# An attention and two-MLP kernel: w3 turned by VectorE and by its store instead of by TensorE, and other sharing of banks and slots in the last stage

## The chip, the cores and the metric

The kernel runs on one NeuronCore of one Trainium2 chip. A core has TensorE (PE, matrix products), VectorE (DVE), ScalarE (ACT), GpSimd (POOL) and SyncE (SP, which here only issues DMAs) and PSUM of eight banks that PE writes and DVE and ACT read. Sixteen DMA engines move data between HBM and SBUF. The metric is device time of one execution in microseconds (us).

## The reference

```python
# q, k, v: 4 x 8 heads x 576 x 64; a causal window of 64 keys
x = softmax(q k^T / 8, windowed) v        # -> 2304 tokens x 512
g = x @ w_gate; v = x @ w_val             # 512 x 1536 each
x = (silu(g) * v) @ w_out                 # 1536 x 512 -> 2304 x 512
a = x @ w1; b = x @ w2                    # 512 x 1024 each
out = ((a * b) @ w3) @ w_out2             # 1024 x 1024, then 1024 x 512
```

The weights come as 64-bit floats and are made 32-bit ones on the chip. The product of the last line is computed as (a * b) @ (w3 @ w_out2), so that w3 meets the 2304 tokens in no product: w34 = w3 @ w_out2 is 1024 x 512.

## The kernel before

**Number format.** Every operand of a matmul is two words, a rounded one (hi, cast on ACT, L197) and the remainder (lo, a subtraction on DVE, L201), and every product takes three passes: hi x hi, hi x lo, lo x hi (`PASSES`).

**Stages in order of time** (the profile's clock): attention (to about 120 us); the first gated MLP; `project`, the product with w_out, in three groups of 768 tokens (PE from 385 to 535 us, three groups of equal work; groups change at 435 and 485 us); the second gated stage (a and b); and `final` from 711 us, the only stage whose code changes, though its weight w3 is prepared earlier.

**How w3 is prepared.** `Plain` (L1012 on) loads 128 rows of w3 in 64-bit form (`st_w`, 1 MB), four instructions for each half narrow it (DVE L185, DVE L187, ACT L189, DVE L191), an ACT copy (L1030) takes the result into a tile `by_w` of 128x512, and a DMA (L1049) stores it to a scratch in HBM, `w3d`. There are eight such row blocks, each in two halves. Four blocks are prepared in `project` (stores at 435, 457, 462 and 468 to 470 us), four in the second gated stage (582 to 648 us). All DMAs are issued by SP, in one queue, in program order; each waits for the one eight before it.

**The first half of `final`: w34.** For each of eight row blocks i (order 0, 4, 1, 5, ...) `transposes(n)` loads the block from `w3d` (L758, two DMAs of 256 KB), turns it on PE against the identity (L771, eight 128x128 pieces into three banks `w3p`), casts it from PSUM on ACT (L773) and takes the remainder on DVE (L774). `row(n)` then runs 24 matmuls of 128x512 (L883, `acc`) of the turned block against the tiles z0h to z7l (w_out2 in two words, sixteen loads of 256 KB, L750). Block n + 1 is turned before row n, so two blocks are turned ahead of the first row. `Right` makes operands of the result: sums and words of the pieces of w34, for seven products.

**The second half of `final`: the output.** For each of three groups of 768 tokens (`Group`), seven products in the order 1, 2, 5, 6, 7, 4, 3 (`PRODUCTS`, a Strassen-Winograd scheme) of 36 matmuls of 128x256 (L948) each, 12 for each of three 128-token tiles t. Products 1, 6, 7 and 4 go into the banks `al` (one for each t), product 2 into `ga` and products 5 and 3 into `be`. After product 1 each `al` is copied to SBUF by ACT (L918); after product 2 each `ga` is added by DVE (L922, 128x256); after 6, 7 and 4 ACT copies `al` again, and after 7 and 3 DVE adds `be`. `ga` has three results in two banks: t = 0 and 1 share one bank, t = 2 has the other. The left operands `hf` of product p and piece m are made by `Left` from the loaded h tiles: for products 5, 6, 7 and 4 first a DVE subtraction in place (L205), then cast (L197) and remainder (L201). `Left` of the next group is queued at product 5.

**What sets the order.** A planner (`Plan`) writes each engine's instructions in a fixed order while the kernel is built. It keeps its own clock with costs such as `dve(n) = 0.16 + 0.00104 n` us, and emits a queued job on an engine when its inputs are due by that clock. `plan.slots` counts free SBUF slots; a job that needs one waits in the queue until `slots` exceed `plan.keep`. On the chip each engine runs its instructions in the written order and waits by semaphores: an instruction that is late holds up everything written behind it on its engine.

Of the kernel before, what the change touches and what calls it, by code (L numbers as in the profile page):

```python
# [16 lines left out]
P = 128  # L17
# [15 lines left out]
def window_attention_moe_kernel(ctx: ExitStack, tc: tile.TileContext, q, k, v, w_gate, w_val, w_out, w1, w2, w3, w_out2, out):  # L33
# [702 lines left out]
    def final(rows, ident):  # L736
# [4 lines left out]
        zt, w3t, w3T = {}, {}, {}  # L741
# [11 lines left out]
        def queue_w3(n):  # L753
            i = ROWS[n]
            for x in range(2):
                def load(eng, x=x):
                    w3t[i, x] = slot([P, 512], F32, f"w3_{i}_{x}")
                    eng.dma_start(out=w3t[i, x], in_=w3d[i][:, 512 * x:512 * x + 512])  # L758
                jobs["w3", i, x] = loading(load, [done[n - 3]] if n > 2 else (), 1)

        def transposes(n):
            i = ROWS[n]
            w3T[i] = []
            for x in range(2):
                plan.need(jobs["w3", i, x])
            for g in range(0, NI, 3):
                n_ = min(3, NI - g)
                pt = bank(f"w3p{i}_{g}")[:, :n_ * P]
                for c in range(n_):
                    at = divmod((g + c) * P, 512)  # L770
                    nc.tensor.transpose(pt[:, c * P:c * P + P], w3t[i, at[0]][:, at[1]:at[1] + P], ident)  # L771
                t = slot([P, 2, T], F32R, f"w3T{i}_{g}")
                nc.scalar.copy(out=t[:, 0, :n_ * P], in_=pt)  # L773
                nc.vector.tensor_tensor(out=t[:, 1, :n_ * P], in0=pt, in1=t[:, 0, :n_ * P].bitcast(F32), op=ALU.subtract)  # L774
                plan.charge("ACT", act(n_ * P))
                plan.charge("DVE", dve(n_ * P))
                w3T[i].append(t)
            plan.slots += 2
            reach(done[n])
# [52 lines left out]
        class Left:  # L832


            def __init__(self, tp):
# [35 lines left out]
                def gone(eng):  # L871
                    plan.slots += NI
                plan.job(gone, [j for x in last.values() for j in x], SP=0.0)
# [3 lines left out]
        def row(n):  # L877
            i = ROWS[n]
            acc = bank(f"acc{i}")
            for c in range(NI):  # L880
                for k, (x, y) in enumerate(PASSES):
                    plan.need(jobs["z", c, y])
                    nc.tensor.matmul(acc, lhsT=w3T[i][c // 3][:, x, (c % 3) * P:(c % 3) * P + P], rhs=zt[c, y],  # L883
                                     start=c == k == 0, stop=c == NI - 1 and k == 2)
                plan.advance(0.68)
            right.put(i, acc)
# [15 lines left out]
        class Group:  # L902
# [28 lines left out]
            def product(self, p):  # L931
# [3 lines left out]
                if p == 1:  # L935
                    self.al = [bank(f"al{self.tp}_{t}")[:, :N2] for t in range(3)]
                elif p == 2:
                    two, one = bank(f"ga{self.tp}_0"), bank(f"ga{self.tp}_1")
                    self.ga = [two[:, :N2], two[:, N2:], one[:, :N2]]
                elif p == 5:  # L940
                    self.be = [bank(f"be{self.tp}_{t}")[:, :N2] for t in range(3)]
# [30 lines left out]
        def run():  # L972
            transposes(0)
            for n in range(NI):
                if n + 1 < NI:
                    transposes(n + 1)
                if n == 3:
                    left[0] = Left(0)
                row(n)
            plan.slots += 2 * NI  # L980
            plan.keep = 6
            for tp in range(NTP):
                group = Group(tp)
                for p in PRODUCTS:
                    if p == 5 and tp + 1 < NTP:
                        left[tp + 1] = Left(tp + 1)
                    group.product(p)
# [29 lines left out]
    class Plain(Doubles):  # L1017
# [6 lines left out]
        def make(self):  # L1024
            for j, ready in enumerate(self.narrowed()):
                t = []

                def copy(eng, j=j, t=t):
                    t.append(large([P, 512], F32, f"by_{self.name}_{j}"))
                    eng.copy(out=t[0], in_=halves(self.st[:, 512 * j:512 * j + 512])[1].bitcast(F32))  # L1030
                a = plan.job(copy, [ready] + by[-2:-1], ACT=act(512))
                self.last.append(a)
                by.append(plan.job(lambda eng, j=j, t=t: self.put(eng, self.n, j, t[0]), [a], lag=5.0, SP=0.5))
# [6 lines left out]
    w3d = [dram.tile([P, DF2], F32, name=f"w3d_{i}") for i in range(DF2 // P)]  # L1040
# [7 lines left out]
    def put_w3(eng, i, j, t):  # L1048
        eng.dma_start(out=w3d[i][:, 512 * j:512 * j + 512], in_=t)  # L1049
# [125 lines left out]
    with tc.manual_schedule():  # L1175
        attention(during_attention)
        ident2 = own.tile([P, P], F32, name="ident2")
        nc.gpsimd.memset(ident2, 1.0)
        nc.gpsimd.affine_select(out=ident2, in_=ident2, pattern=[[-1, P]], compare_op=ALU.is_equal, fill=0.0,
                                base=0, channel_multiplier=1)  # L1180
# [8 lines left out]
        begin_e, run_e = final(rows2, ident2)  # L1189
# [39 lines left out]
```

## Time and profile before

| | |
|---|---|
| median of 3 runs | 864.48 us (863.35 to 864.81) |
| the profiled execution | 863.41 us, of which the span from the first to the last instruction is 861.7 us |
| granted TensorE clock, mean over the span | 0.998 of full speed |
| PE busy | 831.9 us, 97% of the span |
| DVE, ACT, POOL busy | 636.9 us (74%), 458.2 us (53%), 86.0 us (10%) |
| DMA queue | 135.29 MB, 47.7% of 16 engines over the span |

An engine's busy time is the union of its instructions; matmuls are pipelined, so one matmul is in flight longer (334 ns for one of 128x384) than the time between two (about 172 ns). "Idle before, releaser" says which instruction ended a wait. The chain of waits follows the run back from its last instruction; where a stage's chain holds only PE, that stage takes as long as its matmuls.

### The profile page before, as it was taken

Reading aid. Unit: us, or ns where it says so; the run is one execution under the profiler, and the core shown is the slowest. Engines: PE = TensorE matmul, PEld = TensorE weight load, DVE = VectorE, ACT = ScalarE, POOL = GpSimd, SP = SyncE. Lnnn points to the kernel's source line nnn. Section 1 sums busy time; section 2 is a strip of 40 time slices with the busy share of each in tenths; the row PEclk is TensorE's granted clock in tenths of the full one; section 3 lists DMA queues with packets and bytes.
Section 4 is the critical chain, followed back from the end, with each engine's and each line's share of the span. In section 5 each row is a group of like instructions: output and inputs, shape, how many; then the busy total and the mean of one; then the engine's idle time right before and its main releaser. Section 6 shows DMA issues by size and latency. Waiting matters only on the chain.

```text
span 861.7 us, 15759 instructions
## 1 busy us (share of the span) xinstructions
PE 831.9 (97%) x5934; PEld 798.3 (93%) x5934; DVE 636.9 (74%) x1332; ACT 458.2 (53%) x1192; POOL 86.0 (10%) x119
## 2 busy tenths in 40 slices
PE   7899888899999999999999999999999999999998
PEld 6777677899999999999999999999999998899998
DVE  4899968878688767875797683877788645688683
ACT  6888855564646464643565543445454424556362
POOL 3688930000000000000000000000000000000000
PEclk9999999999999999999999999999999999999999
DMA  9979200135255324599997341023545179042422
GB/s 201 221 164 198 80 1 38 41 123 185 108 194 209 143 79 178 184 349 391 384 329 233 135 125 46 37 86 111 196 159 195 50 251 383 1 147 75 147 75 74
DMA packets 109756, 136.30 MB, mean 158 GB/s; under 512 B 61424, under 2 KB 72432, under 8 KB 108656
## 3 DMA queue, kind: packets, MB, share of 16 engines
q1 hardware_dynamic: 109680, 135.29, 47.7%
q8 instruction: 47, 0.77, 0.4%
q14 instruction: 29, 0.24, 0.1%
HBM read 92.27 MB, written 42.99 MB: 157 GB/s over the span
## 4 chain that ended last, share of the span: by engine, by line
PE 80%; DVE 8%; DMA 4%; ACT 2%; SPq 2%; issue 2%; POOL 2%; POOLq 0%; ACTq 0%; DVEq 0%
PE ala L578 14%; PE alb L578 14%; PE o L718 14%; PE beb L578 7%; PE bea L578 7%; PE al L948 6%; PE acc L883 5%; PE gab L578 4%; PE gaa L578 3%; PE be L948 3%; DMA zd<-by_z 2%; PE ga L948 1%; DVE ptt L449 1%; SPq L347 1%; DMA st_z<-in_moe_w_out_dram 1%
## 5 line engine op out<-in xcount | busy, mean ns | idle before, releaser
L718 PE MATMUL o<-ph,wo 128*128 128x384 f32 x576 | 146.5, 334 | 0.2 <-DVE X L705 0.2
L718 PEld LDWEIGHTS o<-ph,wo 128*128 128x128 f32 x576 | 104.1, 188 | 0.5 <-ACT by_w L1030 0.5
L718 PE MATMUL o<-pl,wo 128*128 128x384 f32 x288 | 96.2, 334 | 0.0
L585 ACT COPY ha<-ala 128x384 f32<-128x384 f32 x90 | 42.8, 478 | 54.8 <-PE ala L578 53.3
L589 DVE TENSOR_TENSOR ha<-ha,bea 128x384 f32<-128x384 f32 x60 | 33.2, 554 | 46.4 <-PE bea L578 27.1
L718 PEld LDWEIGHTS o<-pl,wo 128*128 128x128 f32 x288 | 54.1, 188 | 0.0
L424 ACT ACTIVATE pexp<-S,stat 128x128 f32<-128x128 f32 x144 | 51.8, 397 | 0.0
L197 ACT CAST hf<-h 128x384 fp32r<-128x384 f32 x84 | 39.0, 518 | 19.0 <-DVE h L205 18.9
L599 ACT ACTIVATE ha<-ha 128x384 f32<-128x384 f32 x54 | 28.3, 526 | 38.4 <-DVE ha L589 38.4
L201 DVE TENSOR_TENSOR pl<-pl,ph 128x768 fp32r<-128x768 f32 x36 | 33.8, 956 | 19.1 <-ACT ph L197 18.8
L434 POOL TENSOR_TENSOR pexp<-pexp,stat 128x384 f32<-128x384 f32 x48 | 44.4, 944 | 26.7 <-DVE stat L431 21.7
L201 DVE TENSOR_TENSOR hf<-h,hf 128x384 fp32r<-128x384 f32 x84 | 43.2, 554 | 3.4 <-ACT hf L197 3.3
L197 ACT CAST ph<-pl 128x768 fp32r<-128x768 f32 x36 | 29.2, 838 | 27.8 <-DMA pl<-h 20.8
L585 ACT COPY c12b<-alb 128x384 f32<-128x384 f32 x30 | 14.4, 481 | 49.4 <-PE alb L578 49.2
L589 DVE TENSOR_TENSOR c22b<-c22b,beb 128x384 f32<-128x384 f32 x30 | 16.6, 555 | 26.4 <-ACT c22b L585 26.2
L424 ACT ACTIVATION_READ_ACCUMULATOR pexp<-S,stat 128x1 f32 x144 | 33.9, 236 | 0.0
L417 DVE TENSOR_REDUCE stat<-S 128x3 f32<-128x384 f32 x48 | 24.3, 546 | 6.2 <-PE S L410 6.1
L578 PE MATMUL ala<-xo,w_g_1h 128*128 128x384 f32 x120 | 27.0, 337 | 1.7 <-ACT w_g_1h L197 1.7
L463 PEld LDWEIGHTS PV<-ptt,v 128*64 128x64 f32 x576 | 19.5, 137 | 9.2 <-DVE ptt L449 4.5
L463 PE MATMUL PV<-ptt,v 128*64 128x64 f32 x576 | 22.9, 228 | 5.1 <-DVE ptt L449 4.0
L918 ACT COPY o<-al 128x256 f32<-128x256 f32 x36 | 13.4, 373 | 26.3 <-PE al L948 24.9
L201 DVE TENSOR_TENSOR xo<-X,xo 128x384 fp32r<-128x384 f32 x37 | 22.6, 641 | 5.6 <-ACT xo L197 5.6
(546 smaller groups left out, 2524.4 us busy)
## 6 DMA issues: line engine op xcount, KB each, us to landing
h<-ha SPq DMA_DIRECT2D x60, 384.0 KB, 3.2
pl<-h SPq DMA_DIRECT2D x36, 384.0 KB, 6.4
h<-h SPq DMA_DIRECT2D x24, 384.0 KB, 4.8
st_w<-in_moe_w_dram SPq DMA_DIRECT2D x8, 1024.0 KB, 6.8
st_g<-in_moe_w_gate_dram SPq DMA_DIRECT2D x6, 1024.0 KB, 5.6
st_v<-in_moe_w_val_dram SPq DMA_DIRECT2D x6, 1024.0 KB, 5.4
st_wo<-in_moe_w_out_dram SPq DMA_DIRECT2D x6, 1024.0 KB, 5.3
wo<-by_wo SPq DMA_DIRECT2D x12, 512.0 KB, 3.7
```

The source lines that it names most:

```text
L197: (eng.copy if eng is nc.scalar else eng.tensor_copy)(out=hi(), in_=src())
L201: return plan.job(lambda eng: eng.tensor_tensor(out=lo(), in0=src(), in1=hi().bitcast(F32), op=ALU.subtract), after, slots=slots, DVE=dve( ...
L424: nc.scalar.activation(out=pe[:, jj, :], in_=so[:, jj, :], func=AF.Exp, bias=st[:, 0, x, jj:jj + 1], accum_out=st[:, 1, x, jj:jj + 1])
L434: nc.gpsimd.tensor_tensor(out=pe, in0=pe, in1=st[:, 3, x, :].unsqueeze(2).to_broadcast([P, SUB, P]), op=ALU.mult)
L463: nc.tensor.matmul(pp[64 * h:64 * h + 64, 64 * (SUB * x + jj):64 * (SUB * x + jj) + 64], lhsT=vt[u][e][:, at, h, :], rhs=t[:, x, jj, c:c + ...
L578: nc.tensor.matmul(acc, lhsT=self.wt.ops[p, x][:, m, :], rhs=self.xs.ops[p, m][:, y, :], start=start and n == 0, stop=n == 5, skip_group_c ...
L585: nc.scalar.copy(out=out, in_=src)
L589: nc.vector.tensor_tensor(out=out, in0=x, in1=y, op=ALU.add)
L599: nc.scalar.activation(out=h, in_=src, func=func)
L718: nc.tensor.matmul(acc[m, x], lhsT=wos.tiles[i // 6][:, i % 6, :], rhs=rows[2 * tp + x].words(f, b), start=f == n == 0, stop=f == NF - 1 a ...
L883: nc.tensor.matmul(acc, lhsT=w3T[i][c // 3][:, x, (c % 3) * P:(c % 3) * P + P], rhs=zt[c, y], start=c == k == 0, stop=c == NI - 1 and k == 2)
L948: nc.tensor.matmul(acc, lhsT=self.xs.ops[p, m][:, x, t * P:t * P + P], rhs=right.ops[p, m, y], start=start and n == 0, stop=n == 3 * R - 1 ...
```

## The change

1. w3 is turned as it is prepared: the ACT copy into `by_w` becomes a DVE transpose of 128x512 that turns each 32x32 square in itself (L1022 of the new kernel), and the store (L1042) puts the squares in their turned places: four DMAs for each half, each of 64 KB in 512 runs of 128 bytes (one run is one row of a square), into rows of 4096 bytes of one 1024x1024 scratch. Before it was one DMA of 256 KB for each half, in runs of 2048 bytes.
2. In `final` the loads (L762) bring the turned block straight into the operand's slot, three DMAs of 192, 192 and 128 KB for each row block in runs of 512 bytes; the cast and the remainder are now queued jobs (L197, L201) that read SBUF. The 64 transposes on PE, their banks, and the identity that POOL made for them are gone.
3. `ga`: t = 0 and t = 2 share one bank, t = 1 has the other.
4. `Left` gives its slots back in two halves and not all at once, the next group's `Left` is queued at product 6 and not 5, and `plan.keep` is 3 and not 6 in the products.
5. The planner counts 2.0 us of SP and 6.0 us of landing for a store of w3, before 0.5 and 5.0.

```diff
-    def final(rows, ident):
+    def final(rows):
...
         def queue_w3(n):
+
             i = ROWS[n]
-            for x in range(2):
-                def load(eng, x=x):
-                    w3t[i, x] = slot([P, 512], F32, f"w3_{i}_{x}")
-                    eng.dma_start(out=w3t[i, x], in_=w3d[i][:, 512 * x:512 * x + 512])
-                jobs["w3", i, x] = loading(load, [done[n - 3]] if n > 2 else (), 1)
-
-        def transposes(n):
-            i = ROWS[n]
-            w3T[i] = []
-            for x in range(2):
-                plan.need(jobs["w3", i, x])
+            w3T[i] = [None] * -(-NI // 3)
             for g in range(0, NI, 3):
-                n_ = min(3, NI - g)
-                pt = bank(f"w3p{i}_{g}")[:, :n_ * P]
-                for c in range(n_):
-                    at = divmod((g + c) * P, 512)
-                    nc.tensor.transpose(pt[:, c * P:c * P + P], w3t[i, at[0]][:, at[1]:at[1] + P], ident)
-                t = slot([P, 2, T], F32R, f"w3T{i}_{g}")
-                nc.scalar.copy(out=t[:, 0, :n_ * P], in_=pt)
-                nc.vector.tensor_tensor(out=t[:, 1, :n_ * P], in0=pt, in1=t[:, 0, :n_ * P].bitcast(F32), op=ALU.subtract)
-                plan.charge("ACT", act(n_ * P))
-                plan.charge("DVE", dve(n_ * P))
-                w3T[i].append(t)
-            plan.slots += 2
-            reach(done[n])
+                k = min(3, NI - g)
+
+                def load(eng, g=g, k=k):
+                    t = w3T[i][g // 3] = slot([P, 2, T], F32R, f"w3T{i}_{g}")
+                    eng.dma_start(out=t[:, 1, :k * P].bitcast(F32).rearrange("p (c f) -> p c f", c=k),
+                                  in_=w3d[P * g:P * (g + k), P * i:P * i + P].rearrange("(c p) f -> p c f", p=P))
...
+                a = loading(load, [done[n - 3]] if n > 2 else (), 1)
+                b = cast(lambda word=word: word(0), lambda word=word: word(1).bitcast(F32), [a], k * P, 0)
+                jobs["w3", i, g // 3] = rest(lambda word=word: word(1), lambda word=word: word(1).bitcast(F32),
+                                             lambda word=word: word(0), [b], k * P)
...
                 def gone(eng):
-                    plan.slots += NI
-                plan.job(gone, [j for x in last.values() for j in x], SP=0.0)
+                    plan.slots += R
+                for p in (4, 3):
+                    plan.job(gone, [j for (q, m), x in last.items() if q in (7, p) for j in x], SP=0.0)
...
                     two, one = bank(f"ga{self.tp}_0"), bank(f"ga{self.tp}_1")
-                    self.ga = [two[:, :N2], two[:, N2:], one[:, :N2]]
+                    self.ga = [two[:, :N2], one[:, :N2], two[:, N2:]]
...
-            plan.keep = 6
+            plan.keep = 3
             for tp in range(NTP):
                 group = Group(tp)
                 for p in PRODUCTS:
-                    if p == 5 and tp + 1 < NTP:
+                    if p == 6 and tp + 1 < NTP:
                         left[tp + 1] = Left(tp + 1)
...
-                    eng.copy(out=t[0], in_=halves(self.st[:, 512 * j:512 * j + 512])[1].bitcast(F32))
-                a = plan.job(copy, [ready] + by[-2:-1], ACT=act(512))
+
+                    eng.transpose(out=t[0], in_=halves(self.st[:, 512 * j:512 * j + 512])[1].bitcast(F32))
+                a = plan.job(copy, [ready] + by[-2:-1], DVE=dve(512))
...
 def put_w3(eng, i, j, t):
-        eng.dma_start(out=w3d[i][:, 512 * j:512 * j + 512], in_=t)
+        for a in range(P // 32):
+            eng.dma_start(out=w3d[512 * j:512 * j + 512, P * i + 32 * a:P * i + 32 * a + 32].rearrange("(b p) f -> p b f", p=32),
+                          in_=t[32 * a:32 * a + 32].rearrange("p (b f) -> p b f", f=32))
```

The written order moves with it, at three places that matter below. The first is DVE in `project`, where the first group of tokens ends (435 us in the profile of before): `st_w` is the block of w3 being narrowed, `pl` and `ph` are left operands of `project`, and the four L705 copies empty banks `o` that PE needs for the next group. Before, and then now:

```order
L201 TENSOR_TENSOR pl_1_0_5210<-pl_1_0_5210,ph_1_0_5290 128x768
L185 TENSOR_SCALAR st_w_5217<-st_w_5217 128x512 x2
L187 SCALAR_TENSOR_TENSOR st_w_5217<-st_w_5217 128x512 x2
L191 SCALAR_TENSOR_TENSOR st_w_5217<-st_w_5217 128x512 x2
L705 COPY X_0_0_4921<-o_0_0_4925 128x384
L705 COPY X_0_1_4922<-o_1_0_4927 128x384
L705 COPY X_0_2_4923<-o_2_0_4929 128x384
```

```order
L201 TENSOR_TENSOR pl_1_0_5200<-pl_1_0_5200,ph_1_0_5280 128x768
L185 TENSOR_SCALAR st_w_5207<-st_w_5207 128x512 x2
L187 SCALAR_TENSOR_TENSOR st_w_5207<-st_w_5207 128x512 x2
L191 SCALAR_TENSOR_TENSOR st_w_5207<-st_w_5207 128x512 x2
L1022 STREAM_TRANSPOSE by_w_0_5318<-st_w_5207 128x512
L1022 STREAM_TRANSPOSE by_w_1_5320<-st_w_5207 128x512
L705 COPY X_0_0_4911<-o_0_0_4915 128x384
L705 COPY X_0_1_4912<-o_1_0_4917 128x384
```

Two transposes now stand between the narrowing and the copies that empty the banks.

The second is DVE in the products of the first group of `final`, from product 7 to product 4: `hf_4m` are the operands of product 4, `o_1t` the additions of `be` after product 7. Before, and then now:

```order
L201 TENSOR_TENSOR hf_40_8795<-h_0_4_8254,hf_40_8795 128x384
L205 TENSOR_TENSOR h_0_7_8284<-h_0_7_8284,h_0_3_8279 128x384
L922 TENSOR_TENSOR o_10_8756<-o_10_8756,be_0_8675 128x256
L201 TENSOR_TENSOR hf_33_8640<-h_0_7_8284,hf_33_8640 128x384
L922 TENSOR_TENSOR o_11_8774<-o_11_8774,be_1_8676 128x256
L922 TENSOR_TENSOR o_12_8791<-o_12_8791,be_2_8677 128x256
L201 TENSOR_TENSOR hf_41_8843<-h_0_5_8264,hf_41_8843 128x384
L201 TENSOR_TENSOR hf_42_8845<-h_0_6_8274,hf_42_8845 128x384
L201 TENSOR_TENSOR hf_43_8848<-h_0_7_8284,hf_43_8848 128x384
```

```order
L201 TENSOR_TENSOR hf_40_8718<-h_0_4_8226,hf_40_8718 128x384
L205 TENSOR_TENSOR h_0_6_8244<-h_0_6_8244,h_0_2_8238 128x384
L201 TENSOR_TENSOR hf_41_8740<-h_0_5_8233,hf_41_8740 128x384
L916 TENSOR_TENSOR o_10_8685<-o_10_8685,be_0_8618 128x256
L201 TENSOR_TENSOR hf_42_8744<-h_0_6_8244,hf_42_8744 128x384
L205 TENSOR_TENSOR h_0_7_8254<-h_0_7_8254,h_0_3_8250 128x384
L916 TENSOR_TENSOR o_11_8713<-o_11_8713,be_1_8619 128x256
L201 TENSOR_TENSOR hf_33_8583<-h_0_7_8254,hf_33_8583 128x384
L201 TENSOR_TENSOR hf_43_8776<-h_0_7_8254,hf_43_8776 128x384
L916 TENSOR_TENSOR o_12_8738<-o_12_8738,be_2_8620 128x256
```

The operands of product 4 no longer stand behind the last addition after product 7.

The third is SP's queue ahead of the first row of w34: `z4h` to `z7l` are loads of w_out2, `h` the stores of the second gated stage. Before, and then now:

```order
L750 DMA z4l<-zd_121 128x512
L750 DMA z5h<-zd_122 128x512
L750 DMA z5l<-zd_122 128x512
L649 DMA h_3_1_103<-ha_1_0_7645 128x768
L649 DMA h_3_1_103<-ha_1_1_7646 128x768
L750 DMA z6h<-zd_123 128x512
```

```order
L750 DMA z4l<-zd_121 128x512
L649 DMA h_3_1_103<-ha_1_0_7683 128x768
L649 DMA h_3_1_103<-ha_1_1_7684 128x768
L750 DMA z5h<-zd_122 128x512
L750 DMA z5l<-zd_122 128x512
L750 DMA z6h<-zd_123 128x512
```

The loads of z5 stand behind two stores that they stood ahead of; z6 and z7 keep their place.

## Rows read from the trace of the kernel before

**Rows 1.** The page's first part: busy time, share of the span, instructions of each engine.
```profile
PE 831.9 (97%) x5934; PEld 798.3 (93%) x5934; DVE 636.9 (74%) x1332; ACT 458.2 (53%) x1192; POOL 86.0 (10%) x119
```

**Rows 2.** The chain of waits through `final`: start, duration (both us), what ran.
```profile
711.37 1.75 PE w3p L771 x16
...
718.62 0.87 PE w3p L771 x8
719.49 5.49 PE acc L883 x24
...
766.48 1.45 PE ga L948 x12
...
767.95 0.43 DVE o L922
...
768.42 3.14 PE ga L948 x24
...
775.88 4.33 PE al L948 x36
...
781.67 3.27 PE al L948 x25
...
785.36 0.42 DVE o L922
785.78 0.56 DVE hf L201
...
786.39 4.20 PE al L948 x31
...
808.64 8.65 PE al L948 x72
...
818.75 4.19 PE al L948 x31
...
853.94 4.33 PE be L948 x36
```

**Rows 3.** DVE instructions by form, 400 to 711 us: shape, count, busy us, mean ns.
```profile
L187 DVE SCALAR_TENSOR_TENSOR st_w<-st_w 128x512 int32<-128x512 int32 x16 | 10.6, 690 | 0.0
...
L185 DVE TENSOR_SCALAR st_w<-st_w 128x512 int32<-128x512 int32 x16 | 6.2, 425 | 0.0
...
L201 DVE TENSOR_TENSOR pl<-pl,ph 128x768 fp32r<-128x768 f32 x30 | 28.1, 957 | 15.2 <-ACT ph L197 14.9
```

**Rows 4.** DVE over time, 428 to 455 us: start, duration, instructions in a run.
```profile
434.91 1.95 DVE L705 COPY X<-o 128x384 f32<-128x384 f32 x4
...
451.29 1.83 DVE L201 TENSOR_TENSOR pl<-pl,ph 128x768 fp32r<-128x768 f32 x2
```

**Rows 5.** PE over time, 435 to 440 us; in brackets its wait.
```profile
435.61 0.41 PE L718 MATMUL o<-ph,wo 128*128 128x384 f32 x1 [0.17 <-DVE X L705]
```

**Rows 6.** The last load ahead of the first row, tile z7l: starts and landing in us.
```profile
L883 PEld LDWEIGHTS acc<-z7l,w3T x8: 187/188/188, 717.8 to 761.3; 128*128 128x128 f32 x8
...
L750 SPq DMA_DIRECT2D z7l<-zd x1: 353/353/353, 709.3 to 709.3; - x1
...
DMA to landing us min/median/max: 6.3/6.3/6.3
```

**Rows 7.** The DMA queue, 0 to 57 us: packets, MB, share of 16 engines.
```profile
q1 hardware_dynamic: 37904, 11.24, 99.3%
```

**Rows 8.** Windows: length, busy PE, PEld, DVE, ACT, POOL, PE clock, DMA share, GB/s.
```profile
420.00:450.00 30.00, 29.83 (x173) 29.48 (x172) 26.46 (x47) 19.09 (x35) 0.00 (x0) 1.00 1.00 356
450.00:480.00 30.00, 30.00 (x175) 30.00 (x174) 22.50 (x38) 16.62 (x27) 0.00 (x0) 1.00 0.72 249
480.00:510.00 30.00, 30.00 (x175) 30.00 (x174) 21.61 (x44) 14.97 (x31) 0.00 (x0) 1.00 0.37 115
...
762.00:858.30 96.30, 93.42 (x757) 91.37 (x755) 69.38 (x152) 46.83 (x115) 0.00 (x0) 1.00 0.32 113
```

**Rows 9.** SP over time, 425 to 530 us: the store of the second block.
```profile
457.14 0.93 SPq L1049 DMA_DIRECT2D w3d<-by_w  x2
```

More of the change, by code (lines that the diff above doesn't have):

```diff
@@ L740, in final @@
         ROWS = [R * (n % 2) + n // 2 for n in range(NI)]
-        zt, w3t, w3T = {}, {}, {}
+        zt, w3T = {}, {}
         done = [mark() for i in range(NI)]
@@ L754, in queue_w3, with word @@
             i = ROWS[n]
-            for x in range(2):
-                def load(eng, x=x):
-                    w3t[i, x] = slot([P, 512], F32, f"w3_{i}_{x}")
-                    eng.dma_start(out=w3t[i, x], in_=w3d[i][:, 512 * x:512 * x + 512])
-                jobs["w3", i, x] = loading(load, [done[n - 3]] if n > 2 else (), 1)
-        def transposes(n):
-            i = ROWS[n]
-            w3T[i] = []
-            for x in range(2):
-                plan.need(jobs["w3", i, x])
-            for g in range(0, NI, 3):
-                n_ = min(3, NI - g)
-                pt = bank(f"w3p{i}_{g}")[:, :n_ * P]
-                for c in range(n_):
-                    at = divmod((g + c) * P, 512)
-                    nc.tensor.transpose(pt[:, c * P:c * P + P], w3t[i, at[0]][:, at[1]:at[1] + P], ident)
-                t = slot([P, 2, T], F32R, f"w3T{i}_{g}")
-                nc.scalar.copy(out=t[:, 0, :n_ * P], in_=pt)
-                nc.vector.tensor_tensor(out=t[:, 1, :n_ * P], in0=pt, in1=t[:, 0, :n_ * P].bitcast(F32), op=ALU.subtract)
-                plan.charge("ACT", act(n_ * P))
-                plan.charge("DVE", dve(n_ * P))
-                w3T[i].append(t)
-            plan.slots += 2
-            reach(done[n])
+            w3T[i] = [None] * -(-NI // 3)
+            for g in range(0, NI, 3):
+                k = min(3, NI - g)
[3 more added lines that the diff above has]
+                                  in_=w3d[P * g:P * (g + k), P * i:P * i + P].rearrange("(c p) f -> p c f", p=P))
+                def word(x, g=g, k=k):
+                    return w3T[i][g // 3][:, x, :k * P]
+                a = loading(load, [done[n - 3]] if n > 2 else (), 1)
+                b = cast(lambda word=word: word(0), lambda word=word: word(1).bitcast(F32), [a], k * P, 0)
+                jobs["w3", i, g // 3] = rest(lambda word=word: word(1), lambda word=word: word(1).bitcast(F32),
+                                             lambda word=word: word(0), [b], k * P)
         class Right:
@@ L882, in row @@
                     plan.need(jobs["z", c, y])
+                    plan.need(jobs["w3", i, c // 3])
                     nc.tensor.matmul(acc, lhsT=w3T[i][c // 3][:, x, (c % 3) * P:(c % 3) * P + P], rhs=zt[c, y],
@@ L885, in row @@
                 plan.advance(0.68)
+            reach(done[n])
             right.put(i, acc)
@@ L972, in run @@
         def run():
-            transposes(0)
             for n in range(NI):
-                if n + 1 < NI:
-                    transposes(n + 1)
                 if n == 3:
@@ L1029, in copy @@
                     t.append(large([P, 512], F32, f"by_{self.name}_{j}"))
-                    eng.copy(out=t[0], in_=halves(self.st[:, 512 * j:512 * j + 512])[1].bitcast(F32))
-                a = plan.job(copy, [ready] + by[-2:-1], ACT=act(512))
+                    eng.transpose(out=t[0], in_=halves(self.st[:, 512 * j:512 * j + 512])[1].bitcast(F32))
+                a = plan.job(copy, [ready] + by[-2:-1], DVE=dve(512))
                 self.last.append(a)
-                by.append(plan.job(lambda eng, j=j, t=t: self.put(eng, self.n, j, t[0]), [a], lag=5.0, SP=0.5))
+                by.append(plan.job(lambda eng, j=j, t=t: self.put(eng, self.n, j, t[0]), [a], lag=6.0, SP=2.0))
     NF2, NI2 = DF // 256, DF2 // 256
@@ L1039, in window_attention_moe_kernel @@
     zd = [dram.tile([P, 2, DM], F32, name=f"zd_{f}") for f in range(DF2 // P)]
-    w3d = [dram.tile([P, DF2], F32, name=f"w3d_{i}") for i in range(DF2 // P)]
+    w3d = dram.tile([DF2, DF2], F32, name="w3d")
     def put_wo(eng, f, t):
@@ L1176, in window_attention_moe_kernel @@
         attention(during_attention)
[L1177 to L1180, printed above, removed]
         plan.shut.add("POOL")
@@ L1188, in window_attention_moe_kernel @@
         on(events2, len(order2) - 6, lambda: make_to(w3s[-1]))
-        begin_e, run_e = final(rows2, ident2)
+        begin_e, run_e = final(rows2)
         def put_all():
```

## The prediction

> **What bounds the kernel now.** I read first the busy times: PE works in 97% of the span, DVE in 74%, ACT in 53% [rows 1]. So nearly all time is PE's, and an edit pays only where it takes PE's instructions away or ends one of PE's few waits. Then I followed the chain of waits through `final` [rows 2]. The reader is to see two things there. In the first half the chain holds nothing but PE: rows of 24 matmuls (5.49 us) alternate with transposes (0.87 us), without a gap, so each transpose is on the path. In the second half a product of 36 matmuls takes 4.32 to 4.33 us where nothing disturbs it (the row at 853.94), but in places the chain leaves PE for additions and remainders on DVE. Last I read the places outside `final` where the change adds work: DVE and PE around 435 us [rows 4, 5], and the DMA queue [rows 6 to 9].
>
> **The change, part by part.**
>
> *Transposes off PE: -7.0 us.* One piece of two blocks takes 1.75 us, six pieces of one block 0.87 (0.87 or 0.88 each; one of them is shown) [rows 2]: 1.75 + 6 x 0.87 = 6.97 us. All of it is on the path, so all of it goes, provided that something else isn't late. What could be late is the turned operand, now made by a load, a cast and a remainder from SBUF. The casts and remainders are as many as before and of the same size; only their place in the order is new. Block n + 3 is loaded once row n is done, so it has two rows, 2 x 5.49 = 11 us, for a landing of some 6 us (that of z7l in the same queue is 6.3, [rows 6]) and a cast and remainder of three tiles, which overlap (about 2 us, at some 0.5 us each by half of the 957 ns of 128x768, [rows 3]). About 2 us are left; I cost it at nothing and make its failure a rival.
>
> *Product 2, order of `ga`: -2.3 us.* The first 12 matmuls of `ga` take 1.45 us, then PE waits for the addition by DVE (767.95, 0.43 us), because t = 1 writes into the bank that this addition reads [rows 2]. From 766.48 to 768.42 + 3.14 = 771.56 product 2 takes 5.08 us, against 4.32 undisturbed: 0.76 lost; the other two groups have the same break (the first is shown), 2.3 us together. Now t = 1 has a bank of its own and t = 2 comes 12 matmuls (1.44 us, a third of 4.32) after t = 0 ends, when the 0.43 us addition has long been done. Should DVE be a whole microsecond behind, it would still fit.
>
> *Products 7 and 4: -3.1 us.* In group one, product 6 ends at 775.88 + 4.33 = 780.21 and product 4 at 786.39 + 4.20 = 790.59; two products take 10.38 us instead of 8.64, 1.74 lost. The second half of the loss is plain in the chain: DVE adds `be` of the last t at 785.36 and only then makes the remainder of the operand that PE waits for (785.78, 0.56 us), because it is written in this order. In group two, 808.64 to 818.75 + 4.19 = 822.94 is 14.30 us for three products of 4.32, 1.34 lost [rows 2]; in the third group the chain shows nothing lost. 1.74 + 1.34 = 3.1 us. In the new order the operands of product 4 stand ahead of the last addition, and the next group's `Left`, queued one product later, leaves DVE freer before. What is late next: nothing that I see, since DVE is busy in 69.4 of the stage's 96.3 us [rows 8]; if half of it stays, 1.5 us come back. Slots in halves and the lower `keep` only let jobs be written earlier, and carry no price of their own.
>
> *The transpose on DVE: +1.3 us.* Sixteen instructions of 128x512. The trace has no such instruction; the bounds are 0.43 us (the fastest one of that shape, L185) and 0.96 us (half as wide again, the 128x768 `pl`), and I take the 0.69 us of L187, same shape, same engine [rows 3]. Sixteen make 11 us of DVE, of which nearly all lies beside PE. One pair doesn't: at the change of groups the two turns now stand ahead of the copies that empty the banks (434.91, four in 1.95 us), and PE already waits there, 0.17 us, for the first copy [rows 4, 5]. So PE waits for both turns: 2 x 0.69 less an overlap of about 0.07, 1.3 us (0.8 to 1.9 by the bounds). At the change at 485 us DVE reaches its copies early and the pair is hidden. ACT loses its sixteen copies, for which I count nothing.
>
> The Trainium skill, "VectorE: DVE Perf Modes", section "The three transpose paths", gives 311 ns for 128x128 in bf16 on VectorE against 390 on TensorE, and its "Rules for kernel authors" advise TensorE where the result may go to PSUM. An estimate from this page is 4 x 311 = 1.24 us for a turn, 1.2 us more at 435 us than I take, and the sum would be 855.0. No run here shows it so far. The trace speaks against the page's advice in this place: eight TensorE turns cost PE 0.87 us each time, on the path.
>
> *The loads ahead of row 0: +0.4 us.* z7l is issued at 709.3, lands 6.3 us later at 715.6, and is used at 717.8: 2.2 us to spare [rows 6]. Row 0 now starts 1.75 us earlier, so 0.45 is left. Ahead of z7l stand two turned blocks, 1 MB in runs of 512 bytes (128 for each DMA engine) in place of 2048. At the 356 GB/s of a full queue 1 MB takes 2.9 us [rows 8]; if a run of 512 bytes costs twice a packet of 256 (below, 24 ns), 6.1. So z7l is 0 to 3.2 us later and PE loses 0 to 2.7; I take a delay of 0.85, a loss of 0.4, near the lower end because the queue has gaps in which the first of these loads go.
>
> *The stores in runs of 128 bytes: 0.* One block is 4096 runs, 256 for each of the 16 engines, where before it was 512 KB in 1.5 us at 356 GB/s. The nearest row is the loading of q and k in packets of 64 floats: 37904 packets in 57 us at 99.3% are 57000 x 16 x 0.993 / 37904 = 24 ns of an engine for each [rows 7]. Bounds: half of it for half the bytes, 12 ns; 2.5 times, 60 ns, since these are writes and nothing in the trace writes so small. I take 24: a block is 6.1 us, 4.6 more than before. The first block falls at 435 us, when the queue is full (share 1.00, [rows 8]); behind it stand operands for pair 3 of `project`, whose remainder is done at 451.29 + 1.83 = 453.1 [rows 4]. A group of `project` is 50 us, a pair a sixth, 8.3, so PE wants it at 435.4 + 25 = 460.4: 7.3 us to spare against 4.6. The next three blocks go from 457.14 on [rows 9], for the next group's operands wanted from 485 us; the queue there is free 28% and 63% of its time [rows 8], some 8 + 19 = 27 us against 3 x 4.6 = 14. Hidden, then, with a margin that the rival below uses up.
>
> **Sum.** 863.41 - 7.0 - 2.3 - 3.1 + 1.3 + 0.4 = 852.7 us by the profiled execution; the median of before is 1.07 above that execution, so the forecast is **853.8 us**. By the bounds of its terms (turns 0.8 to 1.9, z 0 to 2.7, last stage -5.4 to -3) this case alone lies between 851 and 858.
>
> **Rivals.**
>
> *DVE is late again in the products.* For it: `final` gets the same DVE work in less time, and several additions now stand among the operands. Against: the additions follow PE, and the wait of product 2 is ended by a bank, not by speed. If all 5.4 us of waits stay, 863.41 - 7.0 + 1.7 + 1.07 = 859.2 us.
>
> *Rows wait for the turned operand.* The transposes' time returns as waits for a remainder that stands too late in DVE's order: up to the six rows from n = 2 on, 0.9 us each, 5.4 us: 859.2 us as well. For it: the margin of 2 us out of 11 worked out above. Against: PE's old transposes were free to run a block ahead, and so are these jobs.
>
> *The small stores choke the queue (the slower side).* With t the cost of a run on an engine, the first block delays pair 3 by 256t - 1.5, and PE loses what exceeds 7.3 us: from t = 34 ns. The next three blocks delay pair 2 of the next group, wanted at 485.5 + 16.7 = 502.2. From 457.14 to there are 45 us; cast and remainder take 3, the other loads ahead of it (two of 1 MB, six of 384 KB) 12.5 at 356 GB/s, so 29.6 are left for 768t: from t = 39 ns PE loses 768t - 29.6. The two losses aren't added, since PE late by the first wants the second later. The gain of 10.7 us is gone at t = 53 ns; at 60 it is 863.4 - 10.7 + 16.5 + 1.1 = 870.3 us. Against: 24 ns in the nearest row. For: that row is reads, these are writes of half the size, 4096 bytes apart.
>
> If a store this small has to read before it writes, it takes two accesses of 24 ns, t = 48, a loss of 7.3 and 861.1 us. The Trainium skill states such a rule in "DMA: Bandwidth & Descriptors", section "Specifications" (below 512 bytes a read-modify-write); no row of this trace shows a write that small.
>
> **How the numbers follow.** Forecast 0.60, DVE late in the products 0.17, rows waiting 0.10, small stores 0.13 (half of it up to 862, half beyond). A measurement of this kernel tells 0.2%, 1.7 us, from no change: faster means below 862.8. The first three cases and half of the fourth are faster; with some of the fourth on the line: faster 0.89, same 0.05, slower 0.06. The range 850.0 to 860.5 holds the forecast's case and the two at 859.2, and leaves out the worst of the stores and a gain beyond what the rows carry.
>
> **What would show it.** Right: no `w3p` on PE and rows of `acc` every 5.5 us without gaps; 21 x 4.32 = 90.7 us from the first product to the end of PE's work instead of 96.3 [rows 8]; a wait of about 1.4 us at 435 for DVE's copies; a turn of 0.7 us; landings of the small stores of 2 to 6 us. Wrong: waits of rows for `w3T`; `ga` still waiting for an addition; `project` longer than 150 us by more than 2, with waits for `pl`; a DMA share of 1.00 from 457 to 485.

## The result, and the profile after

The changed kernel takes 853.79 us in the median of 4 runs (852.04 to 856.34), before 864.64 (863.35 to 867.58): a ratio of 0.9862, 95% interval 0.9822 to 0.9903. Forecast were 853.8 us, faster. The profiled execution fell from 863.41 to 852.04 us, its span from 861.65 to 849.79: 11.9 us less. PE is busy in the same share of a shorter span (answers to [rows 1]):

```profile
PE 822.4 (97%) x5870; PEld 790.3 (93%) x5870; DVE 646.2 (76%) x1348; ACT 448.8 (53%) x1176; POOL 85.7 (10%) x117
```

The chain of waits through `final`, start, duration and what ran, answers to [rows 2]:

```profile
711.18 5.93 DMA z7l<-zd
...
717.15 38.83 PE acc L876 x170
755.99 4.31 PE al L942 x36
760.30 4.32 PE ga L942 x36
764.62 4.32 PE be L942 x36
768.94 12.96 PE al L942 x108
...
842.38 4.33 PE be L942 x36
```

The reader is to see that the transposes between the rows are gone, that products 2, 7 and 4 now take 4.32 us like the others, and that a load, z7l, has come onto the path in the first row.

To add the parts up I take the starts of matmuls that begin and end a stage in the trace. Up to the first matmul of `project` all these programs do nearly the same, yet that point lies anywhere from 384.4 to 388.7 us in the profiled executions of this study; a difference of a few us in whole times is therefore no finding, and stages are compared instead. "products" runs from the first to the last start of a product's matmul. Each ratio is against the runs of before that were taken beside that kernel (4 to 21 of them, medians 864.49 to 865.05 us). The three kernels in which the stores choke the queue come at the end.

| kernel | median us (runs) | ratio to before, 95% | project | second gated stage | rows of w34 | products |
|---|---|---|---|---|---|---|
| before | 864.64 (4) | | 150.19 | 175.66 | 50.79 | 95.98 |
| changed | 853.79 (4) | 0.9822 to 0.9903 | 150.75 | 175.66 | 44.51 | 90.59 |
| e1 ga | 862.59 (10) | 0.9954 to 0.9991 | 149.97 | 175.65 | 50.79 | 93.66 |
| e2 left | 860.37 (4) | 0.9914 to 0.9962 | 150.30 | 175.65 | 50.79 | 92.87 |
| e3 turn | 859.51 (6) | 0.9909 to 0.9956 | 149.76 | 175.65 | 44.65 | 96.00 |
| e4 turn, ga | 856.83 (4) | 0.9873 to 0.9923 | 150.83 | 175.63 | 44.64 | 93.67 |
| e5 late turns | 852.76 (4) | 0.9826 to 0.9900 | 149.76 | 175.65 | 44.21 | 90.59 |
| e6 late, z first | 853.17 (4) | 0.9838 to 0.9895 | 149.76 | 175.63 | 44.57 | 90.59 |
| e7 big runs | 855.87 (4) | 0.9838 to 0.9925 | 151.25 | 175.65 | 44.21 | 90.59 |
| e9 product 6 | 862.82 (10) | 0.9971 to 1.0013 | 149.76 | 175.63 | 50.79 | 94.26 |
| e10 slots, keep | 861.16 (10) | 0.9958 to 0.9995 | 149.76 | 175.63 | 50.79 | 92.90 |
| e8 stores twice | 943.65 (4) | 1.0869 to 1.0941 | 199.67 | 215.65 | 44.66 | 90.59 |
| e11 twice, apart | 860.47 (6) | 0.9931 to 0.9966 | 156.04 | 177.34 | 44.38 | 90.59 |
| e12 four, apart | 928.00 (4) | 1.0703 to 1.0757 | 192.69 | 207.81 | 44.44 | 90.59 |

From before to changed: rows of w34 -6.28, products -5.39, `project` +0.56, ahead of `project` -0.44, behind the last matmul -0.30; together -11.85 of the 11.86 us. The 0.56 of `project` lies within what single executions differ by: with the program that the kernel before has in that stage it takes 149.76 to 150.30 us (before, e1, e2, e9, e10), with that of the changed kernel 149.76 to 150.83 (changed, e3, e4). The last two were no part of the reasoning; the 0.30 comes with the turned w3 (3.37 to 3.38 us from the last matmul's start to the end in every such kernel, 3.66 to 3.68 in the others), and I didn't follow it further.

### The profile page after: what moved, and what is told of

It is laid out like the page before. It is cut to its first block, busy times and chain, and to the rows that moved or that the text cites. A ratio compares the mean times of both kernels' runs of the same rounds, so it can differ in the third digit from the quotient of the medians.

```text
span 849.8 us, 15741 instructions
## 1 busy us (share of the span) xinstructions
PE 822.4 (97%) x5870; PEld 790.3 (93%) x5870; DVE 646.2 (76%) x1348; ACT 448.8 (53%) x1176; POOL 85.7 (10%) x117
## 4 chain that ended last, share of the span: by engine, by line
PE 81%; DVE 7%; DMA 4%; SPq 3%; ACT 2%; issue 2%; POOL 1%; POOLq 0%; ACTq 0%; DVEq 0%
PE ala L578 14%; PE alb L578 14%; PE o L718 14%; PE beb L578 7%; PE bea L578 7%; PE al L942 6%; PE acc L876 5%; PE gab L578 4%; PE gaa L578 3%; PE be L942 3%; SPq L347 2%; DMA zd<-by_z 2%; PE ga L942 2%; DVE ptt L449 1%; DMA st_z<-in_moe_w_out_dram 1%
## 5 line engine op out<-in xcount | busy, mean ns | idle before, releaser
L201 DVE TENSOR_TENSOR hf<-h,hf 128x384 fp32r<-128x384 f32 x84 | 43.6, 553 | 5.6 <-ACT hf L197 5.6
L197 ACT CAST ph<-pl 128x768 fp32r<-128x768 f32 x36 | 29.3, 837 | 32.4 <-DMA pl<-h 22.3
L197 ACT CAST hf<-h 128x384 fp32r<-128x384 f32 x84 | 39.3, 514 | 13.0 <-DVE h L205 11.4
L201 DVE TENSOR_TENSOR pl<-pl,ph 128x768 fp32r<-128x768 f32 x36 | 33.4, 952 | 11.8 <-ACT ph L197 11.5
L201 DVE TENSOR_TENSOR xo<-X,xo 128x384 fp32r<-128x384 f32 x37 | 22.6, 641 | 5.7 <-ACT xo L197 5.7
```

Of the source, the lines that this page charges most:

```text
L197: (eng.copy if eng is nc.scalar else eng.tensor_copy)(out=hi(), in_=src())
L201: return plan.job(lambda eng: eng.tensor_tensor(out=lo(), in0=src(), in1=hi().bitcast(F32), op=ALU.subtract), after, slots=slots, DVE=dve( ...
```

## The experiments

**The parts of `final`, one by one.** e1: the order of the `ga` banks alone, put into the kernel before.

```diff
-                    self.ga = [two[:, :N2], two[:, N2:], one[:, :N2]]
+                    self.ga = [two[:, :N2], one[:, :N2], two[:, N2:]]
```

> The kernel before, with the new order of the ga banks alone (t = 0 and 2 share one). Theory 1, each part has its own place: the three waits of ga for the addition go, the stage of products takes 96.0 - 2.3 = 93.7 us, the waits for hf before product 4 stay, span 861.7 - 2.3 = 859.4. Rival, DVE's speed bounds the stage: the wait moves to the next operand on DVE and the stage stays within 0.7 us of 96.0.

The products go from 95.98 to 93.66 us, -2.32, as theory 1 had it. PE's waits for additions into `ga` are gone, those for `hf` are as they were (PE's waits over the run: what waited, for what, us, times, longest):

```profile
PE al L948 <- ACT hf L197: 1.0, 2, 0.5
```

e2: the release of slots, `keep` and the queueing, and not the banks.

```diff
-                    plan.slots += NI
-                plan.job(gone, [j for x in last.values() for j in x], SP=0.0)
+                    plan.slots += R
+                for p in (4, 3):
+                    plan.job(gone, [j for (q, m), x in last.items() if q in (7, p) for j in x], SP=0.0)
-            plan.keep = 6
+            plan.keep = 3
-                    if p == 5 and tp + 1 < NTP:
+                    if p == 6 and tp + 1 < NTP:
```

> The kernel before, with the new release of slots, keep 3 and the next group's operands queued at product 6, and nothing else. Theory 1: the two breaks at products 7 and 4 go (-3.1 us), the three ga breaks stay: 92.9 us for the products, span 858.6. Rival, the breaks of products 7 and 4 came from the ga waits pushing DVE behind: without the bank order they stay and the stage is 95 to 96 us.

The products go from 95.98 to 92.87 us, -3.11, as theory 1 had it, and the waits of PE are the mirror image: the three for `ga` stay, those for `hf` are gone.

```profile
PE ga L949 <- DVE o L923: 1.5, 3, 0.5
```

e3: the changed kernel with all four settings of the products as before; e4: with the new banks alone.

```diff
 # e3 and e4, against the changed kernel
-                    plan.slots += R   (and its two jobs)
+                    plan.slots += NI
-            plan.keep = 3
+            plan.keep = 6
-                    if p == 6 and tp + 1 < NTP:
+                    if p == 5 and tp + 1 < NTP:
 # e3 also
-                    self.ga = [two[:, :N2], one[:, :N2], two[:, N2:]]
+                    self.ga = [two[:, :N2], two[:, N2:], one[:, :N2]]
```

> The changed kernel with the last stage's four old settings (bank order, release of slots, keep, queueing), so only the turning of w3 differs from before. Theory 1: rows of w34 take 44.5 us (as in the changed kernel), the products 96.0 us (as before), span 849.8 + 5.4 = 855.2. Rival, the last-stage settings are needed because DVE has less room after the transposes leave PE: rows wait for the turned operand or the products take 97 us or more, span 857 or more.

> The changed kernel with old release of slots, keep and queueing, but the new bank order. Theory 1, the parts add: products 93.7 us, span 852.9. If the parts overlap, the new bank order alone already brings the products to 91 to 92 us here, or leaves 95.

In e3 the rows take 44.65 us and the products 96.00, in e4 the products take 93.67: the parts add within 0.1 us. The turning of w3 shortens the rows by 6.1 to 6.3 us by itself, and no row waits for its turned operand.

**What ends the breaks at products 7 and 4.** e9 has only the line of product 6 in the kernel before, e10 only the slots and `keep`.

> The kernel before, with the next group's operands queued at product 6 and not 5, and nothing else. In its written order the operands of product 4 (hf_41 to hf_43) still stand behind the last addition after product 7. Theory: that order is the cause of the breaks at products 7 and 4, so at most the first half of the loss in group one goes and the products take 95 us or more. Rival, the next group's operands crowd DVE and that alone is the cause: 93 us.

> The kernel before, with the release of slots in halves and keep 3, and the next group still queued at product 5. In its written order hf_41 to hf_43 stand ahead of the last addition after product 7. Theory: the order is the cause, so nearly all of the 3.1 us goes: products 92.9 to 93.5 us, the three waits of ga stay. Rival: the queueing at product 6 is the cause, 95 us or more.

In e10 the products take 92.90 us, the whole gain. In e9 they take 94.26, less than the 95 that I expected, so queueing at product 6 does half the work. The groups tell why (first start to first start: 32.75 and 32.35 us before, 32.35 and 31.01 in e9, 31.01 and 31.00 in e10). Before, each of the two groups loses 1.35 us in product 4, and group one 0.4 us more in product 7. In e9's written order hf_41 to hf_43 still stand behind the last addition in group one but ahead of all three in group two: the break in product 4 stays in group one and goes in group two, as the order has it. In group three they stand ahead of the additions in before, e9 and e10 alike, and nothing is lost. The chain of e9 in group one, the same two steps as in [rows 2]:

```profile
785.93 0.42 DVE o L922
786.36 0.56 DVE hf L201
```

So the written order is the cause of the two breaks in product 4, and each edit reaches it by another way. The 0.4 us in product 7 have another wait behind them, for an operand (hf_73) whose cast stands behind a copy of `al` on ACT; e9 and e10 both end it, and no run here separates how.

**The turns at the change of groups.** e5 lets the two turns of the first block be written only after the first group of `project`.

```diff
-                a = plan.job(copy, [ready] + by[-2:-1], DVE=dve(512))
+                a = plan.job(copy, [ready] + by[-2:-1] + ([passed[0, DF // P - 1]] if self.n == 0 else []), DVE=dve(512))
```

> The changed kernel, but the two turns of the first block of w3 may be written only after project's first group, so on DVE they stand behind the four copies that empty the banks. Theory: the wait at 435 us (1.0 us between two matmuls in the changed kernel, 0.8 lost) goes, project takes 149.8 to 150.0 us instead of 150.75, and the rest is as in the changed kernel. Rival, the wait comes from the late arrival of the block of w3 and not from the turns: project stays at 150.7.

`project` takes 149.76 us instead of 150.75, with no gap between the matmuls. DVE over time in the changed kernel (answers to [rows 4]) and in e5:

```profile
434.94 1.30 DVE L1022 STREAM_TRANSPOSE by_w<-st_w 128x512 f32<-128x512 f32 x2
436.16 1.91 DVE L705 COPY X<-o 128x384 f32<-128x384 f32 x4
```

```profile
437.20 1.94 DVE L705 COPY X<-o 128x384 f32<-128x384 f32 x4
439.06 1.29 DVE L1022 STREAM_TRANSPOSE by_w<-st_w 128x512 f32<-128x512 f32 x2
```

That agrees with the theory but doesn't decide for it, because in e5 the block of w3 came early as well. Its narrowing on DVE ended 0.83 us ahead of the group's first matmul, in the changed kernel 0.19 us behind it. In e3 it ended 0.87 us ahead, and there `project` takes 149.76 us too, with the turns ahead of the copies.

What shows the part of the turns is the series of executions that have them in front. The gap between the starts of the group's sixth and seventh matmul follows the start of DVE's copies, counted from the group's first matmul, less some 0.3 us: 1.05 us with copies at 1.41 (e4), 1.02 at 1.33 (changed), 0.82 at 1.11 (e11), 0.62 at 0.91 (e12), 0.48 at 0.77 (e7), 0.20 at 0.49 (e8), none at 0.28 (e3; two matmuls are 0.17 apart there as elsewhere). In the changed kernel the copies follow the turns without a pause; without these 1.22 us they would start at 0.11 and the gap would be gone (an estimate from these numbers). So the loss needs both, a late block and turns ahead of the copies.

e6 adds a later load of the second block.

```diff
             queue_w3(0)
-            queue_w3(1)
             for f in range(NI):
                 queue_z(f)
-            for n in range(2, NI):
+            for n in range(1, NI):
                 queue_w3(n)
```

> As the kernel with the late turns, and the second turned block is loaded behind z0 to z7 instead of ahead of them. Theory: z7l lands 1.5 to 2.5 us earlier, no wait before the first row's last matmuls (0.4 to 0.6 us in the changed kernel), the rows of w34 take 43.9 us instead of 44.5, and the second row doesn't wait for its own block; together with the late turns span 848.3. Rival, the second block is then late: rows 45 us or more.

z7l now costs the first row only 0.1 us, but the rows take 44.57 us and not 43.9: the second row waits for its own block. That is the rival's path, at less than the 45 us that it named (PE's waits):

```profile
PE acc L876 <- ACT w3T L197: 0.4, 1, 0.4
```

e5 is 1.0 us shorter in `project` than the changed kernel; the medians, 852.76 and 853.79, can't tell them apart. e6, at 853.17, gains nothing over e5.

**What a store costs.** e7 stores the same number of pieces in long runs, e8 stores each piece twice, e11 and e12 two and four times into scratches of their own.

```diff
 # e7
-            eng.dma_start(out=w3d[512 * j:512 * j + 512, P * i + 32 * a:P * i + 32 * a + 32].rearrange("(b p) f -> p b f", p=32),
-                          in_=t[32 * a:32 * a + 32].rearrange("p (b f) -> p b f", f=32))
+            eng.dma_start(out=w3d[P * i + 32 * a:P * i + 32 * a + 32, 512 * j:512 * j + 512], in_=t[32 * a:32 * a + 32])
 # e8
-        for a in range(P // 32):
+        for a in [x for x in range(P // 32) for _ in range(2)]:
 # e11, e12 (1 or 3 more scratches)
+            for d in [w3d] + more:
+                eng.dma_start(out=d[...], in_=...)
```

> The changed kernel with as many stores of w3 of the same size, but each in 32 runs of 2048 bytes, so that the squares aren't put in their turned places (the output is not the reference's). It prices the runs of 128 bytes. In the changed kernel a run takes 12 to 13 ns of a DMA engine, 3.1 us a block, and the issue of a store takes 0.50 us of SP in the median. Theory 1, the small runs are hidden: landing falls below 2.6 us and the issue of a store to 0.33 us, the time stays within 0.3 us of the changed kernel. Rival, the small stores cost the operands of project something: project is shorter by 0.5 us or more and its wait at 435 is gone.

> The changed kernel with each of the 64 stores of w3 issued twice, so twice the runs of 128 bytes: the price for one block is that of 25 ns a run on the DMA engines, and 16 issues of 0.5 us on SP. By the prediction's formula (a loss from 34 to 39 ns a run on) nothing is lost: project 150.8, span 849.8 to 850.3. Rival, SP's issues and not the DMA engines are the queue's bound: 24 more issues of 0.5 us from 458 to 482 us make the operands of pair 2 12 us later against some 5 us to spare, and project takes 155 us or more.

> The changed kernel with each store of w3 issued a second time into another scratch, so that no store waits for the landing of its twin. Twice the runs: the DMA engines' price is that of 25 ns a run, 6.2 us a block. By the prediction's formula nothing is lost: project 150 to 151 us, span within 0.5 us of the changed kernel. Rival, SP's issues at 0.5 us each are what a store costs: 24 more of them from 458 us make the operands of pair 2 some 12 us later against 5 us to spare, project 155 us or more.

> The same with four stores into four scratches: the price of 49 ns a run on the DMA engines, 12.5 us a block. By the prediction's formula (768t - 29.6) the operands of pair 2 of the last group come 8 us late: project 158 to 160 us, and nothing elsewhere. Rival, 32 issues of 0.5 us a block on SP are the bound: 36 us more from 458 us on, project 172 us or more.

e8 loses 49 us in `project`, part of it at a lower granted clock (mean over the span 0.949), but tells little of the price of a run: its second store writes where the first wrote, so SP waits for the first to land before it issues the second. Eight issues take 11.4 us (SP over time):

```profile
437.68 11.40 SPq L1042 DMA_DIRECT2D w3d<-by_w  x8
```

e7 gains nothing, which speaks for theory 1, though an issue falls only from 0.50 us to 0.42 (0.33 expected) and a landing from 2.6 to 2.2. Its median is 2.1 us longer than that of the changed kernel and not within 0.3, but the two intervals in the table overlap. Its `project` is 0.5 us longer, by waits for `pl` in the first group, ahead of any store; the wait at the change of groups is still there (0.48 us from start to start), so the rival fails. Tile by_w in the changed kernel, then in e7 (ns min/median/max):

```profile
L1042 SPq DMA_DIRECT2D w3d<-by_w x64: 308/500/2266, 435.7 to 652.3; - x64
L1022 DVE STREAM_TRANSPOSE by_w<-st_w x16: 665/702/707, 434.9 to 649.7; 128x512 f32<-128x512 f32 x16
...
DMA to landing us min/median/max: 1.7/2.6/6.7
```

```profile
L1042 SPq DMA_DIRECT2D w3d<-by_w x64: 302/420/1479, 439.9 to 656.0; - x64
...
DMA to landing us min/median/max: 1.6/2.2/6.2
```

e11 decides against the prediction's formula: `project` takes 156.04 us, where it had no loss and the rival 155 or more, and the gated stage 1.7 us more. Most of it doesn't go the way that the rival named, though. DVE and then PE over time at the change of groups in e11:

```profile
487.40 0.71 DVE L1022 STREAM_TRANSPOSE by_w<-st_w 128x512 f32<-128x512 f32 x1 [1.68 <-issue]
491.29 0.71 DVE L1022 STREAM_TRANSPOSE by_w<-st_w 128x512 f32<-128x512 f32 x1 [3.17 <-DMA w3e<-by_w]
491.92 1.91 DVE L705 COPY X<-o 128x384 f32<-128x384 f32 x4
```

```profile
492.50 0.44 PE L718 MATMUL o<-ph,wo 128*128 128x384 f32 x1 [3.18 <-DVE X L705]
```

There are two `by_w` buffers. A turn waits until the stores of two halves back have landed; as the turn now sits on DVE, the copies of the banks wait behind it, and PE behind the copies. Of the 5.3 us that `project` takes more than in the changed kernel, this wait makes 3.5. Another 1.5 are waits for `pl` and `ph` of pair 2 in the last group, the path that the rival named, and 0.5 are waits for `pl` in the first group, ahead of any store; the change at 435 us costs 0.2 less.

Why the stores are slow has two parts. The second block's sixteen issues, with no load among them, take 8.4 us (465.36 to 473.80), one every 0.53 us, while the DMA engines are busy 63% of that time: there SP's issue is the bound. The third block's sixteen take 13.8 us (475.73 to 489.50). In their first part, 475.7 to 482.4, a load of 1 MB and two of 384 KB stand just ahead, the engines are 91% busy, and an issue takes up to 1.6 us. At the second block's pace the third block's last store would have been issued by 484.2 and the turn would not have waited (an estimate, with the landing of 1.9 us). So it is the issues and a full queue together.

In e12 that wait of the turns grows to 21 us, all of it in `project` (DVE's waits, 430 to 580 us):

```profile
DVE by_w L1022 <- DMA w3e<-by_w: 21.3, 3, 8.7
```

and PE waits for operands of `project` as well, the path that the rival named:

```profile
PE o L718 <- ACT ph L197: 10.4, 2, 6.8
```

`project` and the gated stage lose 42 and 32 us, part of it at a lower granted clock (mean over the span 0.959, in the changed kernel 0.998). At 192.69 us `project` is far beyond the 158 to 160 of the formula and lies on the rival's side (172 or more).

## Why the prediction was right, and where it wasn't

The profiled execution came out at 852.04 us, where the sum gave 852.7. That the median meets the forecast to 0.01 us is luck: the four runs spread over 4.3 us, the profiled one is their fastest, two terms of the sum were wrong by 0.6 and 0.7 us in opposite directions, and 0.74 us of the gain (ahead of `project` and behind the last matmul) were in no term.

*Transposes, -7.0:* right, if a little small. Rows and transposes went from 50.79 to 44.51 us. An undisturbed row now takes 5.44 us from its first matmul to the next row's, eight of them 43.52; the other 0.99 are lost at the start (next but one). Without that loss the transposes are worth 50.79 - 43.52 = 7.27 us, and the turned operands are never late.

*`ga`, -2.3, and products 7 and 4, -3.1:* right to 0.1 us, each by itself (e1, e2) and together (e4), and for the reason given: a shared bank, and for product 4 a written order that e9 and e10 show group by group. The 0.4 us of product 7 went too, but that break was not the order of the additions.

*Loads ahead of row 0, +0.4:* the mechanism was right, the size less than half of what came. z7l is issued 1.9 us later and lands 1.5 us later than in [rows 6], where I took 0.85. The first row takes 6.41 us where the others take 5.44, so 0.97 us are lost there, at z6l, z7h and above all z7l. The tile z7l and PE at its first use, in the changed kernel:

```profile
L750 SPq DMA_DIRECT2D z7l<-zd x1: 320/320/320, 711.2 to 711.2; - x1
...
DMA to landing us min/median/max: 5.9/5.9/5.9
```

```profile
717.15 0.50 PE L876 MATMUL acc<-z7l,w3T 128*128 128x512 f32 x1 [0.20 <-DMA z7l<-zd]
```

*The turns at 435 us, +1.3:* mis-sized, 0.56. The turn's price was right (two in 1.30 us). What I missed is that ACT, relieved of its two copies into `by_w`, starts its own copies of banks 1.4 us earlier (434.19 instead of 435.58), and that the banks are handed out in another order. Before, the next group's first three matmuls go into a bank that DVE empties, and the first of them waits for it; in the changed program the first two sets of three go into banks that ACT empties, so that PE ran six more matmuls before it had to wait for DVE. The term supposed the old order of banks. ACT, then PE at its wait, in the changed kernel (the latter answers to [rows 5]):

```profile
434.19 1.60 ACT L702 COPY X<-o 128x384 f32<-128x384 f32 x4
```

```profile
436.74 0.45 PE L718 MATMUL o<-ph,wo 128*128 128x384 f32 x1 [0.68 <-DVE X L705]
```

And the loss isn't fixed, as the series of gaps above shows: in e3, with the same order, the turns began 0.94 us before the group's first matmul and not 0.11 after it, and PE didn't wait at all:

```profile
434.18 1.29 DVE L1021 STREAM_TRANSPOSE by_w<-st_w 128x512 f32<-128x512 f32 x2
435.40 1.91 DVE L705 COPY X<-o 128x384 f32<-128x384 f32 x4
```

*The stores, 0:* the result was right, the argument wrong. I priced a run of 128 bytes at 24 ns of a DMA engine, found 34 to 39 ns to be the edge and 53 the point where the gain is gone. A run costs half of what I took. From 458 to 463 us, when nothing but one block went out (queue: packets, MB, share of 16 engines), it is 5000 x 16 x 0.459 / 3098 = 11.9 ns:

```profile
q1 hardware_dynamic: 3098, 0.39, 45.9%
```

But the engines are idle for half of that window: SP takes 4.96 us to issue the block's eight stores (SP over time, answers to [rows 9]):

```profile
458.26 4.96 SPq L1042 DMA_DIRECT2D w3d<-by_w  x8
```

The formula had no term for the issues, nor for turns that wait for a buffer, and e11, at some 24 ns by that measure, lost 5.3 us of `project` where the formula promised none. The changed kernel stands inside the edge, for none of its turns waits for a store. But the edge lies at less than twice the stores, and not at the three times that 34 to 39 ns would be; how much less, no run shows.

The page "VectorE: DVE Perf Modes" of the Trainium skill ("The three transpose paths") led to an estimate of 1.24 us for a turn; the trace has 0.70, and the measurement decides. (For two turns at 435 us that estimate is 1.1 us more than 2 x 0.69, not the 1.2 of the prediction.) The prediction priced the rule of the Trainium skill in "DMA: Bandwidth & Descriptors" ("Specifications"), a read-modify-write below 512 bytes, at 48 ns a run; stores of 128 bytes took 11.9 ns each. That price was wrong; whether the 11.9 ns hold such a read, no run here shows.

*The rivals.* DVE late in the products and rows waiting for w3T: neither is in the chain. The choked queue is real, by way of `by_w` and the turns more than of late operands, but not at this number of stores.

## What to carry to other kernels

Where the chain of a stage holds PE alone, work taken off PE is worth its time (7.27 us here where the chain held 6.97), and a break in PE whose cause is a shared bank or an instruction written too early on another engine is worth its length to a tenth of a microsecond; such parts add. A wait that depends on when a load arrives is different: it changed from 0 to 1 us between executions of the same instructions, so one execution with the wait gone proves little. Before moving work to an engine that empties PE's banks, list what that work can wait for: here a turn waits for a buffer, the buffer for a store, the store for SP's issue, and all three then stand ahead of the copies. Price many small DMAs by their issue as well as by their bytes and runs, and look at what else is in the queue then.

## What the runs showed of the hardware that was not expected

In a burst of stores of 64 KB in 512 runs, the first issue takes SP 0.31 to 0.33 us where nothing holds it up, as much as one of 256 KB in 128 runs took before; an issue right behind another takes 0.48 us or more (0.50 in the median of all, 0.42 in e7 with 32 runs each), so that eight in a row take 5 us. A run of 128 bytes from SBUF to HBM, 4096 bytes apart, takes 11.9 ns of a DMA engine, half the 24 ns of a 256-byte read in [rows 7]. A turn of 128x512 32-bit words in squares of 32x32 takes 0.70 us, as L187 does on the same shape [rows 3].
